# Newton's step as one chain of three operations, operations tied to engines, and a new table of priorities

## The chip, the cores and the metric

The kernel runs on one core of one Trainium2 chip. The core has a matrix engine (PE, with its weight loads PEld), three engines for elementwise work (VectorE = DVE, ScalarE = ACT, GpSimd = POOL), a queue engine (SP) and DMA engines that move data between HBM and the on-chip memory SBUF; PE writes to another memory, PSUM. The metric is the time of one execution in device microseconds, as the median of several runs.

## What is computed

Three layers follow each other: an attention in which a query sees only the keys of its own hash bucket, a gated block with an RMS norm in front, and a second block with a squared ReLU.

```python
# attention: batch 2, 8 heads, 768 positions, 64 wide; proj is 64 x 6
mask = q_bucket[:, :, :, None] == k_bucket[:, :, None, :]   # 6 sign bits of q @ proj and k @ proj
scores = np.where(mask, scale * q @ k.T, -1e9)
attn = np.exp(scores - max); attn = attn / (sum + 1e-9)
x = attn @ v                                                # 1536 tokens x 512
# first block, 512 -> 1536 -> 512
rms = np.sqrt(np.mean(x * x, axis=-1, keepdims=True) + 1e-06)
xn = x / rms * rms_g
x = (silu(xn @ w_gate) * (xn @ w_val)) @ w_out
# second block, 512 -> 2048 -> 512
out = np.maximum(x @ w_in, 0) ** 2 @ w_out
```

## The kernel before

**Precision and tiles.** Every fp32 factor is held as a high and a low part, and three matmuls (high x high, high x low, low x high) make one product; the `L1164` and `L1277`/`L1291` matmuls are those of the two blocks. The attention has 96 slots, one for each head and each 128 queries: `st_S` (scores, L643, four matmuls of 384 columns), `st_min` (L654, DVE: copies the scores out of PSUM and takes the row's maximum `m`), `st_bias` (L663 on ACT, L665 on DVE: one number per row, `b` from `m`), `st_exp` (L672, ACT), then the high and low halves of the weights, transposed, and `st_PV` (L717). Slots of kind `a` (tiles `Pa`, `hla`, `Ta`) make the high half by `st_hi` (a cast to fp16 in the helper `copy`, L381 on ACT or L383 on DVE), the low half by `st_lo` (helper `sub`, L390, POOL or DVE), and are transposed by a DMA (`st_T`, tile `Ta`). Slots of kind `x` (`Px`, `Tx`) are transposed on PE (`st_TP`, L691).

**The norm.** Slots 0 to 47 are the first batch. Its 768 tokens stand in `xall` in two halves of three tiles (`hf` 0 and 1). For each half `plan_norm` lays out: `squares` (sum of squares into `ss`), `power` (DVE L969, then a power of -0.5 on POOL, L974, into `rr`), four Newton operations (L981, L983, L985, L989, all on DVE, on tiles of 128x3), `scales` (L995 ACT, L997 DVE, L999 POOL), four transposes on PE (`x_pe`, L1007) and for each of them `x_hi` (L1017 ACT, L1019 DVE) and `x_lo` (L394, DVE) into `xT`. Only then can the first product of the gated block, `in_pe`, start. The second batch (slots 48 to 95) goes on while the products of the first run, and its own norm comes later.

**What sets the order.** No order is written by hand. `plan_all` registers 3158 operations with what they read, write and hold, with the engines that may do them (`D`, `A`, `P`, `S`, `T` for PE) and a cost for each; `Plan.run` then takes the operation that can start first by its own estimates, and among equals the one of the lowest rank. A cost that is a pair has a second number: a handicap for that engine. `Plan.shift` moves each rank by an entry of a packed table, `SHIFTS`. `port` says that an operation is kept from running beside one of POOL (or DVE) that has it too. Each engine then runs its operations strictly in the planned order.

The code of the functions that the change touches:

Of the kernel before, what the change touches and what calls it, by code (L numbers as in the profile page):

```python
# [112 lines left out]
H_ACT = 3.0  # L113


SHIFTS = (
# [5 lines left out]
    'wo%0>g<5FG_|LA-xDeSW1?}g(p$GAi@BNL%W&8`Q63s;uUKn|1B-3a%lx)<$R<q?(wi(BIFRPlqquv_6Xy+6kZI_XE_z'
    '82LXl*XCZ#t9A66%te59N50eT&^^HCZ8_>fEIhoiFi2YmvxiFU2^q48Jfp(@nG=;-<n_d?F@NW-Vk5<$dU^@<|%%4{_)'
    'c9>@3buMCg=TrX4%O@!O5EwpFEtQF~FmbY$Nrz5jejiO1gPwj+3dNlGynyP;4gvih{)g(>2hKtAO9J)e2*2ja7v?6<vM'
    '7vRpY;JGo)!?QWZ-1o*@?&_H=;@4i_PVZU2`CY2i(E+NEukkWD?6%X)+0NeJ>Um8u?x^y8shu419k!$XEm}5*qiP*HHV'
    '%-cb%5@W<K2Bik8?V?bh}j?I@oL547XXLd_;)cq1sJCgi*KYD;;<(zIRTvOP#|;#`FZY7%VZHS{aw4O3{JiYWR(-|AVR'
    'rlR$B9^0U`<9YI&v)WiG_c&end?fV>UQO?6*W-uz1@Ac5J=LAp_Ev$u-0xaQvaL#LIy<7zFqRl?{14SrxEkpoONp>Pz{'
    'pSw`E{0~?#Q}EFLX~{mcKdITrG^M`YL~Q^$sbJnJ~|7>$7#HmdUz$FW4o%)ZOHq1oDx4hO<l$+6Vj_)hDRDvCfqyn#hI'
    'hsQXuzXKzz&<!mDbrHDgDJXs*qJtbH@_8vQr9MMB-$xgYqv4Lz7G>}b=!MLi}r_Dq)M8s8Fd@FAA2>My(k;!tD%cGT$d'
    'AOSWhU+A5&3oxB(M!=*&((ev^<+g<4yuv*?$WLW?n+o{R1Bf*$TfNv*Mo_4o_i-=Lf-QnqNT+-ZNEyF{XGNm$NDj?yLQ'  # L130
    'i8R=IFz-(2w!0(t{n+1+3J8vErjHCkPB-SR#)_RFqPb7xt-&`Iyw&@>o;v(W}^jrb5sqCV)9D6gfsYMDRz*P}b~oNObW'
    ';Y!wEw1$+oK7=Q_i%d6CQ7AYW&LS%P#yM|7aSWB$+M#iw_2xk*FOcPn)z0GbC{t|;1_N>8CmEwZ!y#`<s7oLTRnV07Hz'
    'wMHs2u$RGS8*C7L(H?j!c!SojYDPS_CKYdF`ooJ&@sAWEOZ2!+2BprM+A4?SHJb3ycnwhFS7}Gt<?_@24HCp;TD|{NLF'
    '%%)yXv#gVQ4fVJCN3nN)I+0-878lo3i&FMm`Ad=z#$$r<m2>JF_*F?Q9?Q5l4@vOXjL0hRKDq;rh-tt{%yZw#1j+TVFG'
    '}@Zt9&7)DCb}om)ilqn$*#&dbg!8V1FSt}zS)!h=+kKr+CnL7vpK?-N=I3XtOl%%O0zDTiN0D^v=!3FnISpLcy2zI-<q'
    'rR^RkbsW;L-)yQPS>&IED-)6_)0tD0tJS>Z@CYjdEFnab7#58|OzNEiLox)UkKR;Vhp6B{0UY9>*)>S4t=ezOjnA24Vp'
    '3l~kWo&-)7EiW2l-jm5DGPk0qMY98^(0q2W$gQn3f0Z>^rZX^7<k*2}*iX&CK(gC9QS?4L<YeL)8e8-^zE=2oNTRY<gz'
    'lqBY;;jZ(W$_1fkSe9Q3WgANpmt~eb$;{yMs)#>);#C2e==3&STZLbfME3a_u&ByH%bo5R>dtP9>ZKC(%=K%L&-AuC1<'
    'I+L6pchFyh3L0LPFTyWhrFBg5p9y<rEr!-HvNI!FFU|Z4ZqLDP0Hjs1iSQH<;Y5DA#^fJ_uIrKO_R&<z-q&0aXo+Fpy='
    'O|*oWcy8vPq*sG;rxX<MStgpSiqC5t}@xK0Mm(We1Hzpmu$Is%RYh#8f}lkjnx=?AAVc7p`A=XRg3+6B(~uo%11{<Dtc'  # L140
    'udBe#r4sEU!oV^JmakPej8$wUo}RrV6p30|NTdY)cgpR6NniVCnFHsR-y6nn9nVT>`F2J)d38iF^fMr?oJh`uNAO1+P6'
    'I_uRs_P0LPD6WHOJ0$RKDixiN42`@I44^+@fl7C>V2ts3MAv^(ZMBl{2Ro^DM>d8IhYrDTB4C3aN50pmG8dGO*q)A_B%'
    'DUP=p&Yo&v|-zDtoKpBhV3b7eApJp0eKFp4&(xIbyz?PPTiz-qZSaH6BW#eAyGn>p!>>QHnNztVEishkEG?T`SQY{5Bb'
    'kR-@J=MIKc5p(ehE63|KP#c`;+8VOg?X;g*G#sS<7$3mhkK!s{9?turQ9%u=?1usNJ=m+)ie*77}tG)*!mx`uPk<>(S_'
    '+zyePUAF{4686g4RE4-g*vM-csqWgW}#PdJa(ZJ+#ROiztIYLN!G<#s4rATSDe3*6qV(>Fd2=+?a(4o)mdfds$8@KwT5'
    'J9FQc3#Hbq{%8fBv<&`xZzSE2H3DEx`qs)MSE#G(;8B3_B#o#}Qy{u<ii*-+UT#QLKXtT}|#NvNap<P_#oBUE=-49~!W'
# [24 lines left out]

class Op:
# [1364 lines left out]
```

## Time and profile before

| | |
|---|---|
| median of 3 runs | 774.93 us (773.62 to 779.03) |
| the profiled execution | 773.52 us, of which the span from first to last instruction is 771.7 us |
| PE | 755.7 us busy (98%) |
| DVE | 652.1 us (84%) |
| ACT | 452.4 us (59%) |
| POOL | 277.7 us (36%) |
| chain that ended last | PE 86%, ACT 5%, DMA 4%, DVE 3% |

The page also cuts the span into 40 slices of 19.3 us; a digit is the busy share in tenths:

```profile
PE   8889998899999999999999999999999999999998
DVE  8989889989898889999889888997669677697765
ACT  5988999979998785636553344466523243232320
POOL 6787877677887574222102121310000000000000
```

The shares are means over two different stages: in the first seven slices all four engines work on the attention; after that PE holds the products of the two blocks.

### The profile page before, as it was taken

How to read it: one execution, taken by the hardware profiler on the slowest of the kernel's cores; microseconds unless marked ns; L12 is line 12 of the kernel's file. 1: busy time of each engine (PE TensorE's matmuls, PEld its weight loads, DVE VectorE, ACT ScalarE, POOL GpSimd, SP SyncE). 2: the span in 40 equal slices, each digit the busy share in tenths (PEclk: the TensorE clock that was granted, in tenths of full speed). 3: DMA queues.
4: the chain of work that ended last, by engine and by line, in shares of the span. 5: the costliest groups of instructions: out<-in, count | busy, mean ns of one | idle time of the engine just before them, and what ended most of it. 6: DMA issues, size and time to landing. Idle time of an engine off the chain costs nothing.

```text
span 771.7 us, 14424 instructions
## 1 busy us (share of the span) xinstructions
PE 755.7 (98%) x5407; PEld 684.2 (89%) x5407; DVE 652.1 (84%) x1301; ACT 452.4 (59%) x871; POOL 277.7 (36%) x244
## 2 busy tenths in 40 slices
PE   8889998899999999999999999999999999999998
PEld 5778897899999999999999999988888888888886
DVE  8989889989898889999889888997669677697765
ACT  5988999979998785636553344466523243232320
POOL 6787877677887574222102121310000000000000
PEclk9999999999999999999999999999999999999999
DMA  8888967698998976333334244313111131111004
GB/s 258 181 184 168 175 139 169 122 231 202 209 216 180 208 162 165 110 133 141 114 119 137 96 142 147 122 60 132 56 55 54 55 110 54 55 55 55 28 1 163
DMA packets 127769, 99.63 MB, mean 129 GB/s; under 512 B 106436, under 2 KB 109460, under 8 KB 127700
## 3 DMA queue, kind: packets, MB, share of 16 engines
q1 hardware_dynamic: 127028, 97.21, 48.6%
q10 hardware_dynamic: 672, 1.51, 0.8%
q8 instruction: 42, 0.69, 0.4%
q14 instruction: 27, 0.22, 0.1%
HBM read 67.12 MB, written 3.15 MB: 91 GB/s over the span
## 4 chain that ended last, share of the span: by engine, by line
PE 86%; ACT 5%; DMA 4%; DVE 3%; issue 1%; POOL 1%; SPq 0%; ACTq 0%; POOLq 0%; DVEq 0%
PE mo L1164 43%; PE mo L1291 17%; PE mo L1277 13%; PE S L643 6%; PE O L717 4%; DMA Ta<-hla 2%; PE mo L528 1%; ACT Px L672 1%; DMA two<-wv 1%; ACT Tx L381 1%; PE mo L691 1%; ACT Pa L672 1%; PE mo L1007 1%; DMA rk<-in_k 1%; ACT hla L381 0%
## 5 line engine op out<-in xcount | busy, mean ns | idle before, releaser
L1164 PE MATMUL mo<-xTA,wih 128*128 128x384 f32 (+1 forms) x512 | 139.1, 353 | 0.0
L1164 PE MATMUL mo<-xTD,wih 128*128 128x384 f32 (+1 forms) x512 | 136.9, 348 | 0.0
L390 POOL TENSOR_TENSOR hla<-Pa,hla 128x768 f16<-128x768 f32 x66 | 110.7, 1681 | 40.8 <-ACT hla L381 29.1
L1308 DVE TENSOR_TENSOR acc<-acc,mo 128x512 f32<-128x512 f32 (+1 forms) x165 | 100.7, 615 | 21.3 <-PE mo L1291 17.7
L1116 DVE SCALAR_TENSOR_TENSOR wv<-wraw,wv 128x512 uint32<-128x512 uint32 x164 | 112.5, 694 | 1.3
L1164 PEld LDWEIGHTS mo<-xTA,wih 128*128 128x128 f32 x512 | 93.6, 189 | 5.2 <-DVE xTA L394 0.2
L1164 PEld LDWEIGHTS mo<-xTD,wih 128*128 128x128 f32 x512 | 93.4, 188 | 5.0
L1200 ACT ACTIVATE mt<-mo 128x512 f32<-128x512 f32 x48 | 28.7, 597 | 109.8 <-PE mo L1164 109.7
L1164 PE MATMUL mo<-xTA,wil 128*128 128x384 f32 (+1 forms) x256 | 89.9, 351 | 0.0
L1164 PE MATMUL mo<-xTD,wil 128*128 128x384 f32 (+1 forms) x256 | 89.0, 348 | 0.0
L1094 ACT ACTIVATE wv<-wraw 128x512 f32<-128x512 f32 x104 | 68.9, 669 | 25.0 <-DMA wraw<-in_w 24.8
L654 DVE TENSOR_SCALAR_CACHE_REDUCE Pa<-S 128x768 f32<-128x768 f32 x66 | 62.8, 951 | 6.9 <-PE S L643 6.6
L1204 DVE TENSOR_TENSOR mu<-mt 128x512 f32<-128x512 f32 x48 | 33.2, 692 | 38.1 <-ACT mt L1200 38.1
L1277 PE MATMUL mo<-yh,woh 128*128 128x384 f32 x192 | 64.9, 338 | 0.0
L1277 PE MATMUL mo<-yh,wol 128*128 128x384 f32 x192 | 64.3, 335 | 0.0
L1277 PE MATMUL mo<-yl,woh 128*128 128x384 f32 x192 | 64.3, 335 | 0.0
L672 ACT ACTIVATE Pa<-Pa,b 128x768 f32<-128x768 f32 x66 | 62.1, 942 | 2.0
L643 PE MATMUL S<-k,q 128*128 128x384 f32 x192 | 55.4, 370 | 5.6 <-DVE Pa L654 3.6
L381 ACT CAST hla<-Pa 128x768 f16<-128x768 f32 x66 | 55.0, 835 | 3.4 <-DMA Ta<-hla 2.9
L381 ACT CAST wih<-wv 128x512 fp32r<-128x512 f32 x38 | 23.6, 621 | 50.6 <-DVE wv L1116 50.4
L643 PE MATMUL S<-two 76*128 76x384 f32 x192 | 50.6, 345 | 1.8 <-DMA two<-wv 1.8
L1164 PEld LDWEIGHTS mo<-xTA,wil 128*128 128x128 f32 x256 | 48.5, 189 | 2.5
(162 smaller groups left out, 1822.7 us busy)
## 6 DMA issues: line engine op xcount, KB each, us to landing
wraw<-in_w SPq DMA_DIRECT2D x104, 512.0 KB, 4.0
rk<-in_k SPq DMA_DIRECT2D x14, 384.0 KB, 4.8
vr<-in_v SPq DMA_DIRECT2D x8, 384.0 KB, 5.4
out<-acc SPq DMA_DIRECT2D x11, 256.0 KB, 2.0
rq<-in_q SPq DMA_DIRECT2D x13, 192.0 KB, 4.3
two<-q SPq DMA_DIRECT2D x7, 192.0 KB, 4.5
two<-wv SPq DMA_DIRECT2D x15, 72.0 KB
Ta<-hla SPq DMA_TRANSPOSE x66, 4.0
```

Source lines behind the costliest of these rows:

```text
L381: nc.scalar.copy(out_, in_)
L390: engine[eng].tensor_tensor(out=out_, in0=in0, in1=in1, op=ALU.subtract)
L643: nc.tensor.matmul(sp[:, hf, 0:TB], d[a][0:kr, t * 128:(t + 1) * 128], d[b2][0:kr, hf * TB:(hf + 1) * TB], start=(n == 0), stop=(n == 1),)
L654: nc.vector.tensor_scalar(out=e["P"].rearrange("p (a b) -> p a b", a=2), in0=e["sp"][:, :, 0:TB], scalar1=-1e9 / SCALE, scalar2=None, op0= ...
L672: nc.scalar.activation(e["P"], e["P"], AF.Exp, bias=e["b"], scale=SCALE)
L1094: nc.scalar.activation(t, f32(wst[m]["hi"]), AF.Abs)
L1116: nc.vector.scalar_tensor_tensor(out=t, in0=src, scalar=scalar, in1=t, op0=op, op1=ALU.bitwise_or)
L1164: nc.tensor.matmul(ps, a[:, c * 128:(c + 1) * 128], b2[:, c, :], start=(c == 0 and n == 0), stop=(c == 3 and n == 2),)
L1204: nc.vector.tensor_tensor(out=us["u"], in0=st["t"], in1=st["t"], op=ALU.mult)
L1277: nc.tensor.matmul(po, a[:, dc * 128:(dc + 1) * 128], b2, start=(j == 0 and n == 0), stop=(j == len(fs) - 1 and n == 2),)
L1291: nc.tensor.matmul(po, a[:, tt * 128:(tt + 1) * 128], b2[:, cols], start=(j == 0 and n == 0), stop=(j == len(fs) - 1 and n == 2),)
L1308: nc.vector.tensor_tensor(out=ac[:, cols], in0=ac[:, cols], in1=po, op=ALU.add)
```

## The change

- `newton` was four planned operations (three products and one multiply-add, each of its own), which the planner could put apart on DVE. It is now one planned operation that issues three `scalar_tensor_tensor` instructions behind one another; the other three entries are empty, so that the count of entries stays. Its cost in the plan is 0.55 and `port` is off.
- The table has a third byte for each operation: a way. An operation that has one gets no handicap on that engine and 6.0 on any other. It is a preference: 428 operations have one, and 36 of these stand on another engine in the plan that results.
- `st_bias` may go to POOL (with a handicap of 40, so only where the table ties it there).
- The table of priorities is another one.
- `store` is written in another way and issues the same.

```diff
+LAG = 6.0
 SHIFTS = (
-    'c-rlk=XX}c*1-47oadaUC31lvNGMVzh9VsiLJMH%2m}PAgc=ceAt2=nNC{O!?;QkbCV~c(CV@);rDFsIA~iHgo_5ZhGw'
+    'c-rk(cYGDqw%&ExnMp|KNR=uCK?sH-AVox)#2{c0xL!m+r3g}`7!2VVAc!ae29TmCNN*w_Di@`LC@pj)kO)am%FLNFGk'
...
+    def lag(self, o, eng, c):
+        if o.way:
+            return 0.0 if eng == o.way else LAG
+        return c[1] if isinstance(c, tuple) else 0.0
...
             moved = int.from_bytes(raw[2 * n:2 * n + 2], "little", signed=True)
+            way = raw[2 * count + n]
+            o.way = "TDAPS"[way - 1] if way else None
             o.rank = (round(o.rank * 32) + moved) / 32 + n * 1e-6
...
-                        ) + (c[1] if isinstance(c, tuple) else 0.0)
+                        ) + self.lag(o, eng, c)
...
-            nc.vector.tensor_scalar(
+            engine[eng].tensor_scalar(
                 out=e["b"], in0=e["m"], scalar1=-SCALE, scalar2=math.log(PSC), op0=ALU.mult,
...
-        add(lambda e: st_bias(e, i), i + R_BIAS, r=[("m", i)], w=[("b", i)], A=0.105, D=(0.08, H_B))
+        add(lambda e: st_bias(e, i), i + R_BIAS, r=[("m", i)], w=[("b", i)], A=0.105, D=(0.08, H_B), P=(0.15, 40.0), port=False)
...
-    def newton(eng, hf, step):
+    def newton(eng, hf):
         ts = slice(hf * TT, hf * TT + TT)
-        r, n = rr[:, ts], rt[:, ts]
-        if step == 0:
-            nc.vector.tensor_tensor(out=n, in0=r, in1=r, op=ALU.mult)
-        elif step == 1:
-            nc.vector.tensor_tensor(out=n, in0=n, in1=ss[:, ts], op=ALU.mult)
-        elif step == 2:
-            nc.vector.tensor_scalar(
-                out=n, in0=n, scalar1=-0.5, scalar2=1.5, op0=ALU.mult, op1=ALU.add
-            )
-        else:
-            nc.vector.tensor_tensor(out=r, in0=r, in1=n, op=ALU.mult)
+        r, n, x = rr[:, ts], rt[:, ts], ss[:, ts]
+        stt = nc.vector.scalar_tensor_tensor
+        stt(out=n, in0=r, scalar=-0.5, in1=r, op0=ALU.mult, op1=ALU.mult)
+        stt(out=n, in0=n, scalar=1.0, in1=x, op0=ALU.mult, op1=ALU.mult)
+        stt(out=r, in0=n, scalar=1.5, in1=r, op0=ALU.add, op1=ALU.mult)
...
         for n in range(4):
             add(
-                lambda e, n=n: newton(e, hf, n), R_X, r=[("rr", hf)], w=[("rr", hf)], D=0.08,
-                port=n != 2,
+                (lambda e: None) if n else (lambda e: newton(e, hf)), R_X, r=[("rr", hf)],
+                w=[("rr", hf)], **({} if n else dict(D=0.55, port=False)),
             )
```

Three places show what this does to the order. The first is DVE at the first norm, behind the power of half 0. Before (`rt` and `rr` are Newton's tiles, `Pa,m<-S` is `st_min`, `sc`/`ma` belong to the scale of `v`):

```order
L983 TENSOR_TENSOR rt<-rt,ss 128x3
L961 SCALAR_TENSOR_TENSOR wv,ss<-xall 128x512
L605 RECIPROCAL sc<-ma 128x2
L654 TENSOR_SCALAR Pa,m<-S 128x768
L985 TENSOR_SCALAR rt<-rt 128x3
L969 TENSOR_SCALAR ss<-ss 128x3
L989 TENSOR_TENSOR rr<-rr,rt 128x3
L654 TENSOR_SCALAR Pa,m<-S 128x768
L997 TENSOR_SCALAR xall<-xall,rr 128x512
```

The same place now, from the instruction ahead of Newton's first on:

```order
L599 TENSOR_REDUCE mx<-vr 128x1
L999 SCALAR_TENSOR_TENSOR rt<-rr 128x3
L1000 SCALAR_TENSOR_TENSOR rt<-rt,ss 128x3
L1001 SCALAR_TENSOR_TENSOR rr<-rt,rr 128x3
L408 TENSOR_TENSOR Tx<-mo,Tx 128x384
L554 TENSOR_SCALAR wv<-mo,cst 48x384
L408 TENSOR_TENSOR Tx<-mo,Tx 128x384
L672 TENSOR_SCALAR Pa,m<-S 128x768
```

Newton's chain of half 0 now stands closed behind one other operation after the power; before, its first and last step had thirteen rows between them, and three of half 1's four steps stood ahead of the first `x_lo`. Half 1's chain now stands behind the last `x_lo` of half 0.

The second place is POOL at the same power (`rr<-ss,half`). Before:

```order
L390 TENSOR_TENSOR hla<-Pa,hla 128x768
L974 TENSOR_TENSOR rr<-ss,half 128x3
L390 TENSOR_TENSOR hla<-Pa,hla 128x768 x2
L1100 TENSOR_SCALAR wv<-wv 128x512
L385 TENSOR_SCALAR k_2690<-rk 128x768
```

And now (`b<-m` is `st_bias`, `xall<-xall,rr` is `scales`):

```order
L683 TENSOR_SCALAR b<-m 128x1
L992 TENSOR_TENSOR rr<-ss,half 128x3
L408 TENSOR_TENSOR hla<-Pa,hla 128x768
L1011 TENSOR_SCALAR xall<-xall,rr 128x512
L408 TENSOR_TENSOR hla<-Pa,hla 128x768
L683 TENSOR_SCALAR b<-m 128x1
```

A `st_lo` stands directly behind the power in both. One of the three `scales` of half 0 has come to POOL, ahead of the second `st_lo`, and biases stand between.

The third place is DVE in the second batch, some 70 slots into the attention. Before:

```order
L654 TENSOR_SCALAR Pa,m<-S 128x768
L1189 SCALAR_TENSOR_TENSOR mu<-mt,mo 128x384
L665 TENSOR_SCALAR b<-m 128x1
L390 TENSOR_TENSOR q_3923<-rq,q_3923 64x768
L654 TENSOR_SCALAR Pa,m<-S 128x768
L1194 SCALAR_TENSOR_TENSOR mu<-mu,mo 128x384
```

And now (`hla<-Pa` as a CAST is `st_hi`):

```order
L683 TENSOR_SCALAR b<-m 128x1
L401 CAST hla<-Pa 128x768
L1201 SCALAR_TENSOR_TENSOR mu<-mt,mo 128x384
L672 TENSOR_SCALAR Pa,m<-S 128x768
L408 TENSOR_TENSOR two<-rk,k_3887 128x768
L408 TENSOR_TENSOR q_3892<-rq,q_3892 64x768
L672 TENSOR_SCALAR Pa,m<-S 128x768
L401 CAST hla<-Pa 128x768
```

Casts of `st_hi`, which were all on ACT, now stand on DVE too: 13 in the program, 3 of them ahead of the first `in_pe`.

Counted over the program: of the biases 22 go from ACT to POOL and 14 from ACT to DVE; 13 `st_hi` from ACT to DVE; 15 operations of the weights' conversion (`w_f32`) from DVE to POOL and 3 back. Ahead of the first `in_pe` PE has 56 `st_S` (57 before), and as many `st_PV` (52), `st_TP` (60) and `hash_pe` (10) as before.

## Rows read from the trace of the kernel before

**Rows 1.** The core's span and mean granted clock of PE.
```profile
core 0: 771.7 us, clock 0.993
```

**Rows 2.** Windows: stretch, length, busy us of PE, PEld, DVE, ACT, POOL; PEclk, DMA.
```profile
300.00:320.00 20.00, 20.00 (x168) 19.67 (x167) 19.75 (x45) 12.77 (x27) 7.13 (x9) 1.00 0.24 81
...
54.50:123.30 68.80, 67.92 (x925) 60.67 (x926) 61.87 (x152) 63.39 (x135) 53.37 (x42) 1.00 0.81 172
123.30:139.20 15.90, 11.64 (x143) 9.67 (x140) 15.05 (x40) 14.75 (x30) 12.79 (x10) 0.89 0.78 144
139.20:320.00 180.80, 180.79 (x1679) 174.80 (x1680) 162.25 (x330) 149.81 (x297) 121.40 (x99) 0.99 0.85 181
```

**Rows 3.** Chain that ended last: start us, us, what; from the norm on.
```profile
125.87 4.04 DMA Ta<-hla
...
139.21 0.94 PE S L643 x4
140.15 3.47 PE mo L1164 x12
...
159.29 0.70 PE S L643 x4
...
177.61 2.08 PE mo L1164 x12
...
768.40 0.42 DVE acc L1308
```

**Rows 4.** Timeline of DVE between the power and the first product.
```profile
128.34 0.17 DVE L983 TENSOR_TENSOR rt<-rt,ss 128x3 f32<-128x3 f32 x1
128.43 0.68 DVE L961 SCALAR_TENSOR_TENSOR wv<-xall 128x512 f32<-128x512 f32 x1
...
129.98 1.46 DVE L985 TENSOR_SCALAR rt<-rt 128x3 f32<-128x3 f32 x1
...
134.25 0.48 DVE L997 TENSOR_SCALAR xall<-xall,rr 128x512 f32<-128x512 f32 x1
134.65 0.95 DVE L390 TENSOR_TENSOR two<-rk,k 128x768 fp32r<-128x768 f32 x1
135.51 1.63 DVE L985 TENSOR_SCALAR rt<-rt 128x3 f32<-128x3 f32 x1
...
138.11 0.94 DVE L654 TENSOR_SCALAR_CACHE_REDUCE Pa<-S 128x768 f32<-128x768 f32 x1
...
138.99 1.66 DVE L394 SCALAR_TENSOR_TENSOR xTA<-mo,cst,xTA 128x384 fp32r<-128x384 f32 x3
```

**Rows 5.** Timeline of POOL in the same stretch.
```profile
123.33 0.88 POOL L974 TENSOR_TENSOR rr<-ss,half 128x3 f32<-128x3 f32 x1 [1.65 <-DVE ss L969]
...
129.77 1.64 POOL L390 TENSOR_TENSOR hla<-Pa,hla 128x768 f16<-128x768 f32 x1
...
134.68 2.45 POOL L390 TENSOR_TENSOR hla<-Pa,hla 128x768 f16<-128x768 f32 x1 [2.07 <-ACT hla L381]
```

**Rows 6.** Timeline of POOL and of DVE at the second batch's norm.
```profile
288.54 1.66 POOL L390 TENSOR_TENSOR hla<-Pa,hla 128x768 f16<-128x768 f32 x1 [0.40 <-ACT hla L381]
...
289.60 1.16 DVE L961 SCALAR_TENSOR_TENSOR wv<-xall 128x512 f32<-128x512 f32 x1
```

**Rows 7.** Windows of 5 us around the first product.
```profile
135.00:140.00 5.00, 2.66 (x35) 2.55 (x34) 5.00 (x8) 4.35 (x9) 4.92 (x3) 1.00 0.64 149
140.00:145.00 5.00, 5.00 (x23) 4.80 (x23) 4.39 (x10) 4.43 (x9) 2.50 (x3) 0.66 0.61 131
```

**Rows 8.** Instructions by line (ns min/median/max, first and last start), and ACT's longest wait for DVE.
```profile
L383 DVE CAST k<-rk x2: 554/557/560, 5.1 to 90.0; 128x768 fp32r<-128x768 f32 x2
...
L385 POOL TENSOR_SCALAR ones<-vr x8: 507/512/857, 16.5 to 217.1; 128x384 f16<-128x384 f32 x8
L385 POOL TENSOR_SCALAR k<-rk x5: 824/831/1103, 66.7 to 222.4; 128x768 fp32r<-128x768 f32 x5
...
ACT b L663 <- DVE Pa L654: 14.4, 18, 3.2
```

More of the change, by code (lines that the diff above doesn't have):

```diff
@@ L122 @@
[L122 to L146, printed above, removed]
@@ new lines @@
+    '5wY#o{J&ERd_HLlGEYHv7Q$r^1UU(4F(RdT<?x!Or}Bl-iaN6(<k?p1fLw?C{6%ftszS&ga{#n0>vn994crR)t92W#^a'
+    'bR=CSe_?GDFMIvv4QdUom*$0E<S955))ddNc(xAZi3<F>9T$w$o91?7TWNc^N%g#%-gR-BY?I>TNV-vvC%yP4?@F+`He'
+    'Rn0l!7}2QdIPm@|HK>tFB<Rg*uGvmq(h1>?vLoWpC~e!7c7%o<hG-zBgm!4}(`psq7dp(Y*=Fp_=qccC1;=jInpveOP~'
+    'Yl{dg0>JE0Rcx8hNtx%TE(gRHbTkS6HpKdwP-i;E8WH~JxoGo{TGo8;f{dtd}bGb`$t=!YrLdijs+^Xy}j7QzsR5eXK<'
+    'F%w2qN>&0oy+QjW}vk1JU@cI#=Vdq9tXFe<W1s{yp`FH58?4*9yq2LFe><%GnfvQo)-sseUS<l*kRzfSgE|h=U87^WqJ'
@@ new lines @@
+    '9)U}rn%z!S}3^cshGJ*79TnlLNaR*7cE;10GhqbXX+QgYTxL9iLDG(R++Mdjgia?p&F%R}4T8qA`}(oHGF$in^YB-Glf'
+    'AAHFR_r77fr6l?qx`4Cc^L8iagj3(y8z}A0VvD3t=*XN8aDUj7<z?-Zy0b&xGLQ^gg}q;<cKC+iQ}zqyOK>23gKuLU!^'
+    'Q|=MudNikJ>$)Xfwmfa5}kBr6jNl{$dYi*?};xk(bL7*mt3Vj}_I!$3lPL7aN*{N4u2eXpsMeUb81c=>FTOtE~jd?6uO'
+    '{0c5_?2eIv)1`XU#eZ%eQeoLz)*5gmrc&U$a(v!V;T+(a0!$4<mZ0WNwRJ2k~NL#!h?#f261U?UT5gVj&UO(w^c8o7Uf'
+    '3hyhGF(lZ(h{W}-s#Z8;#u|*PoP|kl$tO-%nl#Lr=lpKOFrDltswP~p5P!Xk!<Gmq(fvsS6F-Lah#=0rIqE6@FkR_EEe'
@@ L169 @@
+    'z~W6{08t*E4#p!=e_cXxNI6lr+m?i-{S2X{zC|A7613dzI&oF3Xk`~PYG3&dxk7X'
 )
@@ L250, in shift @@
     def shift(self):
-        raw = zlib.decompress(base64.b85decode(SHIFTS)) if SHIFTS else bytes(2 * len(self.ops))
-        assert len(raw) == 2 * len(self.ops)
+        count = len(self.ops)
+        raw = zlib.decompress(base64.b85decode(SHIFTS)) if SHIFTS else bytes(3 * count)
+        assert len(raw) == 3 * count
         for n, o in enumerate(self.ops):
             moved = int.from_bytes(raw[2 * n:2 * n + 2], "little", signed=True)
+            way = raw[2 * count + n]
+            o.way = "TDAPS"[way - 1] if way else None
             o.rank = (round(o.rank * 32) + moved) / 32 + n * 1e-6
@@ L1323, in store @@
         halves = ((nc.scalar, slice(0, CUT)), (nc.sync, slice(CUT, DM)))
-        for queue, cols in halves if (blk, NF2 - 1, tt) == LAST else halves[1:]:
-            if (blk, NF2 - 1, tt) != LAST:
-                cols = slice(0, DM)
+        for queue, cols in halves if (blk, NF2 - 1, tt) == LAST else ((nc.sync, slice(0, DM)),):
             queue.dma_start(
```

74 lines of the change are left out of this document (48 added, 26 removed).

## The prediction

> **What bounds the kernel now.** I read the span first: 771.7 us in the profiled execution, whose own time is 773.5 us, so 1.8 us lie around it [rows 1]. Then the windows: between 139.2 and 320 us PE is busy 180.79 of 180.80 us, between 54.5 and 123.3 us DVE, ACT and POOL are busy 61.9, 63.4 and 53.4 of 68.8 us, and between 123.3 and 139.2 us PE fills only 11.6 of 15.9 us [rows 2]. Then the chain that ended last: the reader is to see a ramp in which transposing DMAs, DVE, ACT and POOL alternate, and from the scores at 139.21 us on nothing but PE pieces, one ending where the next begins, up to the last accumulation at 768.40 us [rows 3]. So the time is the moment at which PE becomes dense, about 139.2 us, plus the PE work that is still open then. Work of DVE, ACT or POOL behind that moment costs nothing as long as PE never waits for it. PE's instructions are the same before and after but for their order, so the change can act in three ways only: an earlier or later first `in_pe`, other PE work done ahead of it, and stalls in the dense stretch.
>
> **The way from the power to the first product.** POOL's power of half 0 starts at 123.33 us [rows 5], the first product at 140.15 us [rows 3]: 16.8 us. DVE is the engine that ends it, with the last `x_lo` at 140.65 us [rows 4].
>
> What Newton costs there: the multiply-add L985 took 1.46 and 1.63 us, its neighbours of the same 128x3 shape 0.17 us [rows 4]. The row of POOL says why: the first began at 129.98 us while POOL's `st_lo` ran from 129.77 to 131.41 us, and ended at 131.44 us; the second ended at 137.14 us, 0.01 us behind a `st_lo` that ended at 137.13 us [rows 5]. The instruction is held until POOL's is over.
>
> Is the new chain free of that? Its three instructions read two tiles of SBUF each. Such a one is L961: begun at 289.60 us under a `st_lo` that ended at 290.20 us, it ended at 290.76 us and took 1.16 us [rows 6], against 0.68 us elsewhere [rows 4]. So two-input instructions are held too, and since a `st_lo` stands right behind the power on POOL, the chain will meet one. I count three instructions at 0.17 us, 0.5 us, plus a hold of 1.5 us for the first (most of a `st_lo` of 1.64 us); the bounds are 0.5 us without a hold and 0.5 + 3 x 1.64 = 5.4 us if each met one of its own. Behind that `st_lo` POOL's next instruction is a `scales` that waits for the chain, so the second and third meet none.
>
> The Trainium skill says of this, in "Advanced Engine Details and Errata", section "VectorE Performance Modes", that GpSimd and Vector instructions that use both read ports block each other. By that sentence alone, three two-input instructions would not be held, and the sum below would be 1.5 us less. "GPSIMD Engine Reference", section "Key points", names Vector instructions with two SBUF inputs beside those; the trace agrees with this one, by the 1.16 us of L961 [rows 6].
>
> DVE between power and last `x_lo`, new against old: the two L985 go (-3.1 us), five small steps of some 0.1 us each between starts go (-0.5), one `st_min` fewer (-0.95), one `split_k2` fewer (-0.95), one `squares` fewer (-0.7), one `scales` fewer (-0.45), two `x_hi` more at the 0.55 us of a `x_lo` (1.66 / 3) (+1.1), the new chain (+0.5) and its hold (+1.5) [rows 4, 5]: -3.5 us. The `st_hi` cast of slot 53 stands behind the last `x_lo`.
>
> Two more paths have to follow, or DVE waits. ACT: 30 instructions in 14.75 us, 0.49 us each [rows 2]; the order has six fewer, -2.9 us. POOL and its DMA: the last `st_PV` ahead of the first product is slot 51's. POOL's row up to its `st_lo` is power 0.88, `st_lo` 1.64, the wait for Newton until about 3.0 us, `scales` 0.6, `st_lo` 1.64, a bias, a weight's step 0.6, a cast of `k` 0.8 and the `st_lo` 1.64, some 8.5 us [rows 5, 8]; a transposing DMA of 4.04 us [rows 3] and the products give 13.1 us. The three end 13.3, 13.9 and 13.1 us behind the power, where the old one took 16.8 us. I take 13.5 us: **-3.3 us**, with bounds 0 (one of the three late by what the chain loses) and -5 us (no hold).
>
> **Ahead of the power.** Counting the order by engine up to the power: ACT loses 17 biases at 0.1 us and two casts, net some -2.4 us; DVE gains two `st_hi` and a `st_lo`, net some +2.4 us; POOL loses 3 to 4 us of `q`, `v` and `st_lo` work and gets 16 biases. No row has a bias on POOL. POOL's one-input instructions take 512 ns for 384 and 831 ns for 768 columns [rows 8], which leaves some 0.2 us for one column; the power on 3 columns took 0.88 us [rows 5]. I take 0.2 us, 3.2 us in all; even at 0.88 us the 14 us fit in POOL's 15.4 us of idle time [rows 2], though each then holds what is queued behind it. What they save is ACT's standing at a bias until DVE has the maximum: 14.4 us in 18 waits over the program [rows 8]; but the `st_exp` behind still wants the same number. ACT was the fuller engine there (63.4 against 61.9 us [rows 2]) and they trade places: **0 us**, bounds -2.4 and +2.4.
>
> **What is left for later.** One `st_S` fewer stands ahead of the first product: **+0.7 us** [rows 3].
>
> **The dense stretch.** Between the first and the 36th product DVE gets ten casts of `st_hi` (0.56 us each by the cast of `k` [rows 8]), ten biases, three `st_lo`, and gives away `squares`, `scales`, `x_lo` and weight steps: net some +4 us. The casts were planned as if POOL never held them; by POOL's 121 of 181 us [rows 2] two thirds of them would meet a `st_lo`, half of 1.64 us each: +5.5 us. DVE had 18.5 us idle there [rows 2], so 9.5 us fit on average; they don't where it was full already, 19.75 of 20 us at 300 us [rows 2]. **+0.5 us**, bounds 0 and +9.5. Newton's later chains and the other form of the store cost nothing: PE's queue covers the first, and the second issues the same DMAs.
>
> **Sum.** 773.5 - 3.3 + 0.7 + 0 + 0.5 = 771.4 us on the profiled execution's time. That time lies 1.4 us under the median of the three runs, which spread by 5.4 us; by the median the sum is 772.8. I forecast **772 us**.
>
> **Rivals.** *(1) The ramp ends where it did.* The three paths lie within a microsecond of each other, so any one being late takes the gain: a transposing DMA of over 7 us instead of 4.04, or DVE's 2.4 us ahead of the power. For it: the chain shows DVE, ACT and DMA taking turns. Then 773.5 + 0.7 = 774.2, or up to 776 us. *(2) Slower: DVE becomes the bound in the dense stretch.* Its place is 280 to 340 us, where it is all but full; it decides once casts and their holds exceed what was idle there. Price: up to 9.5 us, against a gain of 2.6: 776 to 781 us, 783 at worst with rival 1. Against it: PE lost nothing there with DVE at 90%. *(3) More.* PE's first twelve matmuls took 3.47 instead of 2.08 us and the scores 0.94 instead of 0.70 [rows 3], with a granted clock of 0.66 at 140 to 145 us, part of it at 1.2 instead of 2.4 GHz, behind 5 us in which PE was busy 2.66 [rows 7]. A shorter hole may keep 2.4 GHz: -1.6 us. With ACT's 2.4 us and no hold (-1.5): 766 to 769.5 us.
>
> **How the numbers follow.** Forecast (769.5 to 774 us) 0.48, rival 1 0.18, rival 2 0.14, rival 3 0.20. The range 766.5 to 778.5 us leaves out about half of rival 3's lower end and half of rival 2. A measurement here tells 1%, 7.7 us, from no change: faster than 767.2 us takes some 0.12 out of rival 3, slower than 782.7 us 0.05 out of rival 2; the rest, 0.83, is within.
>
> **What would show it.** The first L1164 matmul at 136 to 137.5 us; Newton's three instructions within 2.5 us, the first long and ending with a `st_lo`; biases on POOL at about 0.2 us; PE without gaps from there on. Wrong would be: a PE wait behind 140 us, a first `st_PV` ahead of `in_pe` that waits for `Ta`, or a power later than 125 us.

## The result, and the profile after

The changed kernel is slower: median 785.32 us (782.43 to 786.58, four runs) against 774.27 us (772.33 to 779.03) of the kernel before on the same chips, a ratio of 1.013 with a 95% interval of 1.0093 to 1.0166. The forecast was 772.0 us, the range 766.5 to 778.5. The profiled execution of the changed kernel took 786.58 us, with a span of 784.8 us.

| | before | after |
|---|---|---|
| span | 771.7 us | 784.8 us |
| first `in_pe` matmul | 139.99 us | 139.96 us |
| span behind it | 631.7 us | 644.8 us |
| PE | 755.7 us (98%) | 761.8 us (97%) |
| DVE | 652.1 us (84%) | 669.8 us (85%) |
| ACT | 452.4 us (59%) | 439.0 us (56%) |
| POOL | 277.7 us (36%) | 286.3 us (36%) |

The first matmul of the first product, before and after (start us, us):

```profile
139.99 0.51 PE L1164 MATMUL mo<-xTA,wih 128*128 128x384 f32 x2
```

```profile
139.96 0.59 PE L1176 MATMUL mo<-xTA,wih 128*128 128x384 f32 x2
```

In these two executions the whole difference of 13.1 us arises behind the first product, where the prediction expected nothing but dense PE work. The span of the changed kernel, and the same windows as in [rows 2, 7] (stretch, its length, then busy us of PE, PEld, DVE, ACT and POOL with instruction counts; PEclk; DMA share; GB/s):

```profile
core 0: 784.8 us, clock 0.989
```

```profile
139.20:320.00 180.80, 172.08 (x1570) 163.85 (x1571) 165.30 (x320) 129.83 (x237) 116.23 (x97) 0.98 0.86 175
```

```profile
140.00:145.00 5.00, 2.29 (x17) 1.97 (x12) 4.93 (x6) 1.66 (x2) 4.84 (x3) 1.00 0.47 90
145.00:150.00 5.00, 3.87 (x17) 3.81 (x18) 3.08 (x7) 4.20 (x7) 2.54 (x3) 0.66 1.01 126
185.00:190.00 5.00, 3.16 (x41) 3.05 (x42) 4.22 (x9) 4.43 (x8) 4.28 (x4) 0.74 1.18 303
```

PE is busy 172.08 of 180.80 us where it was busy 180.79 before [rows 2]: 8.7 us of waits. Beside the longest of them the granted clock is lower: 0.66 behind the hole of 140 to 145 us and 0.74 at the hole of 185 us, so part of that work runs at 1.2 instead of 2.4 GHz. The kernel before had one such stretch, 0.66 behind its own hole ahead of 139.2 us [rows 7]. What PE waited for between 139 and 325 us (sum, times, longest):

```profile
PE S L661 <- DVE Pa L672: 6.1, 5, 3.8
PE O L735 <- DMA Ta<-hla: 2.7, 4, 1.8
```

In the kernel before, the same view of the same stretch has one row, a `st_S` waiting 2.3 us for `st_min` at the very start. The longest wait of the changed kernel stands right behind the first product:

```profile
146.13 0.73 PE L661 MATMUL S<-k,q 128*128 128x384 f32 x2 [3.84 <-DVE Pa L672]
```

The chain that ended last, there (start us, us, what):

```profile
140.80 0.90 DVE hla L401
141.70 1.70 DVE rt L999
143.40 0.02 issue
143.42 0.17 DVE rt L1000
143.62 1.49 DVE rr L1001
145.11 0.89 DVE Pa L672 x2
145.99 0.14 issue
146.13 1.37 PE S L661 x4
```

This is Newton's second chain (half 1), between the `st_hi` cast of slot 53 and `st_min` of slot 55. DVE and POOL side by side (start us, us, engine, line, operation):

```profile
140.72 0.98 DVE L401 CAST hla<-Pa 128x768 f16<-128x768 f32 x1
141.62 1.76 DVE L999 SCALAR_TENSOR_TENSOR rt<-rr 128x3 f32<-128x3 f32 x1
143.42 0.16 DVE L1000 SCALAR_TENSOR_TENSOR rt<-rt,ss 128x3 f32<-128x3 f32 x1
143.62 1.49 DVE L1001 SCALAR_TENSOR_TENSOR rr<-rt,rr 128x3 f32<-128x3 f32 x1
145.03 0.94 DVE L672 TENSOR_SCALAR_CACHE_REDUCE Pa<-S 128x768 f32<-128x768 f32 x1
```

```profile
139.63 1.66 POOL L408 TENSOR_TENSOR hla<-Pa,hla 128x768 f16<-128x768 f32 x1
141.36 2.00 POOL L408 TENSOR_TENSOR q<-rq,q 64x768 fp32r<-64x768 f32 x1
143.45 3.25 POOL L408 TENSOR_TENSOR hla<-Pa,hla 128x768 f16<-128x768 f32 x2
```

The reader is to see two ends that agree and one start. The first instruction of the chain begins 0.26 us into POOL's `q` and ends with it (143.38 and 143.36 us). The second begins 0.03 us ahead of POOL's next instruction and takes 0.16 us. The third begins 0.17 us into that `st_lo`, one of two that take 3.25 us together, 1.63 us each, and ends when it does (145.11 and 145.08 us). Three instructions worth 0.5 us take 3.5 us. All the while PE has run out: the one product that its order has there, the twelve matmuls of 139.96 us, was over at 142.3 us, and the next in its order is a `st_S` that stands behind `st_min` of slot 55. The Trainium skill says of the port that DVE and POOL share, in "SBUF — State Buffer", section "SBUF: two separate sides", that whoever starts first has it for the whole instruction and the other is blocked; the trace agrees, by these ends and by the 0.16 us of the one that started first.

The theory to be tested was therefore: **one block on DVE, the second closed chain under POOL's holds, starves PE**. The rivals: the `st_hi` casts on DVE; the biases on POOL, which would make the transposes and so `st_PV` late; the new order as such; the new form of the step.

### The profile page after: what moved, and what is told of

Read it like the earlier page. It is cut to its first block, busy times and chain, and to the rows that moved or that the text cites. A ratio compares the mean times of both kernels' runs of the same rounds, so it can differ in the third digit from the quotient of the medians.

```text
span 784.8 us, 14382 instructions
## 1 busy us (share of the span) xinstructions
PE 761.8 (97%) x5407; PEld 686.7 (88%) x5407; DVE 669.8 (85%) x1313; ACT 439.0 (56%) x809; POOL 286.3 (36%) x275
## 4 chain that ended last, share of the span: by engine, by line
PE 75%; DVE 10%; DMA 7%; ACT 4%; issue 2%; POOL 2%; SPq 0%; POOLq 0%; DVEq 0%; ACTq 0%
PE mo L1176 38%; PE mo L1303 17%; PE mo L1289 12%; DMA Ta<-hla 5%; PE S L661 4%; PE O L735 3%; DVE Pa L672 2%; DVE Px L672 2%; DMA two<-wv 1%; ACT hla L399 1%; DVE Tx L408 1%; PE mo L546 1%; DMA rk<-in_k 1%; ACT Tx L399 1%; ACT Pa L690 1%
## 5 line engine op out<-in xcount | busy, mean ns | idle before, releaser
L408 POOL TENSOR_TENSOR hla<-Pa,hla 128x768 f16<-128x768 f32 x62 | 103.2, 1668 | 34.2 <-ACT hla L399 25.2
L408 POOL TENSOR_TENSOR wol<-wv,woh 128x512 fp32r<-128x512 f32 x10 | 13.3, 1333 | 108.6 <-ACT woh L399 84.6
L403 POOL TENSOR_SCALAR wih<-wv 128x512 fp32r<-128x512 f32 x10 | 6.8, 682 | 126.0 <-DVE wv L1128 125.3
```

Of the source, the lines that this page charges most:

```text
L408: engine[eng].tensor_tensor(out=out_, in0=in0, in1=in1, op=ALU.subtract)
```

## Experiments

Ratios are to runs of the kernel before on the same chip, with 95% intervals; the changed kernel itself stands at 1.013. The chips differ: the median of the kernel before was 774.27 us beside the changed kernel and 776.17 to 777.55 us beside the experiments. So the ratios are to be compared, and an expectation in microseconds is to be read as a ratio to 774.27. The column "second chain" is the time from the first instruction of Newton's second chain to the end of its last in the profiled execution, where it is closed and on DVE.

| kernel | ratio | interval | second chain |
|---|---|---|---|
| changed kernel | 1.0130 | 1.0093 to 1.0166 | 3.49 us |
| e1_form (old order, new form) | 0.9957 | 0.9933 to 0.9982 | open |
| e2_hi (casts on ACT) | 1.0060 | 1.0031 to 1.0090 | 2.50 us |
| e3_bias (biases on ACT) | 1.0113 | 1.0061 to 1.0164 | 3.49 us |
| e4_chain (chain behind `st_min` 55) | 1.0077 | 1.0052 to 1.0101 | 1.40 us |
| e5_two (e2 and e4) | 1.0105 | 1.0074 to 1.0135 | 2.74 us |
| e6_order (new order, old engines) | 1.0215 | 1.0191 to 1.0239 | 2.66 us |
| e7_engines (old order, new engines) | 1.0348 | 1.0319 to 1.0378 | open |
| e8_pool (Newton on POOL) | 1.0040 | 1.0011 to 1.0069 | on POOL |
| e9_pool_hi (e8 and e2) | 1.0041 | 1.0013 to 1.0069 | on POOL |
| e10_pool (old order, Newton on POOL) | 0.9991 | 0.9964 to 1.0017 | on POOL |
| e11_closed (old order, closed chain) | 1.0025 | 1.0006 to 1.0044 | 0.56 us |
| e12_half1 (second chain alone on POOL) | 1.0047 | 1.0023 to 1.0071 | on POOL |
| e13_again (e1 once more) | 0.9968 | 0.9943 to 0.9994 | open |
| e14_free (nothing on POOL that holds the chain) | 1.0019 | 0.9995 to 1.0043 | 0.98 us |

### The parts, each by itself

**e1_form**: the new form of Newton's step alone.

```diff
     # the kernel before; steps 0, 1 and 3 stay where they were, step 2 issues nothing
-    nc.vector.tensor_tensor(out=n, in0=r, in1=r, op=ALU.mult)
+    stt(out=n, in0=r, scalar=-0.5, in1=r, op0=ALU.mult, op1=ALU.mult)
-    nc.vector.tensor_tensor(out=n, in0=n, in1=ss[:, ts], op=ALU.mult)
+    stt(out=n, in0=n, scalar=1.0, in1=ss[:, ts], op0=ALU.mult, op1=ALU.mult)
-    nc.vector.tensor_scalar(out=n, in0=n, scalar1=-0.5, scalar2=1.5, op0=ALU.mult, op1=ALU.add)
-    nc.vector.tensor_tensor(out=r, in0=r, in1=n, op=ALU.mult)
+    stt(out=r, in0=n, scalar=1.5, in1=r, op0=ALU.add, op1=ALU.mult)
```

> The kernel before with Newton's three-instruction form alone: step 0, 1 and 3 at their old places of the old order, step 2 empty, the old table, no ways. In the kernel before L985 was held twice by POOL (1.46 and 1.63 us) ahead of the first product; the new form has none of it there, but its three two-input instructions can each meet a hold. Theory 'the form is the loss': 780 us or more. Theories that put the loss on place, casts, biases or order: 772 to 774.5 us, ratio to the kernel before 0.997 to 1.000.

773.39 us, ratio 0.9957: the form is not the loss, it comes out as a small gain. At the places where the old order has the steps, none of the six instructions of the first batch is held; the last step of each half, from DVE's timeline:

```profile
131.72 0.15 DVE L986 SCALAR_TENSOR_TENSOR rr<-rt,rr 128x3 f32<-128x3 f32 x1
...
141.23 0.16 DVE L986 SCALAR_TENSOR_TENSOR rr<-rt,rr 128x3 f32<-128x3 f32 x1
```

The same instruction on the same tiles takes 0.15 us or 1.49 us, by what POOL does when it begins.

**e2_hi**: the 13 casts back on ACT, order kept.

```diff
         for o in plan.run():
+            if "st_hi" in o.fn.__code__.co_freevars:
+                o.eng = "A"
             o.fn(o.eng)
```

> The changed kernel, its order kept, with the 13 st_hi casts that had gone to DVE put back on ACT. Theory 'casts make DVE the bound in the dense stretch' (13 x 0.56 us plus some 2.6 us of holds between 140 and 325 us): most of the loss comes back, 775 to 778 us. Theory 'one block, Newton's second chain ahead of st_min 55': only the one cast in that block is taken out, 0.98 us, so 783 to 785 us. Theory 'biases on POOL' or 'the order itself': 783 us or more.

781.40 us, ratio 1.0060: half of the loss comes back, less than the theory of the casts wanted (1.001 to 1.005) and more than a single 0.98 us. The trace shows why the two theories aren't clean here: without the cast in front of it the chain begins while POOL still runs the `st_lo` before, so its held instructions take 0.59 and 1.67 us instead of 1.76 and 1.49, and `st_min` of slot 55 begins 3.6 us behind the first product (142.32 less 138.70) instead of 5.1 (145.03 less 139.96). PE's waits of 139 to 325 us:

```profile
PE O L735 <- DMA Ta<-hla: 4.1, 3, 2.3
PE S L661 <- DVE Pa L672: 3.9, 3, 2.2
```

The wait for `st_min` is smaller, the one for the transposes larger.

**e3_bias**: the same edit with `st_bias` in place of `st_hi`.

> The changed kernel, its order kept, with every bias on ACT (36 had gone to POOL or DVE, some more stood on DVE before). Theory 'biases on POOL delay exp, st_lo and the transposes, so that st_PV waits for Ta (2.7 us of PE waits, four of them)': 780 us or less. Theories of the chain, of the casts or of the order: 784 to 787 us, since ACT then waits at a bias for DVE's maximum as before.

787.22 us, ratio 1.0113: no different from the changed kernel. The biases on POOL are not the cause; waits for the transposes are there without them too (3.0 us against 2.7).

**e4_chain**: `st_min` of slot 55 ahead of the block.

```diff
-        for o in plan.run():
+        order = plan.run()
+        for n in (914, 851):   # st_hi of slot 53, Newton of half 1
+            o = plan.ops[n]
+            order.remove(o)
+            order.insert(order.index(plan.ops[930]) + 1, o)   # behind st_min of slot 55
+        for o in order:
```

> The changed kernel with one place of its order changed: on DVE st_min of slot 55 goes ahead of Newton's second chain (three instructions, 3.4 us with holds) and of the st_hi cast of slot 53 (0.98 us). Theory 'one block': PE's wait of 4.05 us at 142 to 146 us and the half clock behind it (some 1.7 us) go, 779 to 781 us. Theory 'casts' or 'order': the gap is only moved, since DVE stays behind through 140 to 310 us, 784 us or more.

783.45 us, ratio 1.0077: the 779 to 781 us of the first theory are 1.006 to 1.009, so it holds by the ratio, but the mechanism is not quite as told. `st_S` waits less now (0.38 us at 143 us), but the chain, still held for 1.01 us, is later, and the next to wait is PE's transposition `x_pe` of half 1, for ACT's scales behind the chain (1.7 us at the longest):

```profile
PE mo L1019 <- ACT xall L1007: 1.9, 2, 1.7
PE S L661 <- DVE Pa L672: 1.9, 3, 1.3
```

So two kinds of work on PE wait for the block: `st_S` by way of `st_min`, and `x_pe` by way of the scales. Changing the place makes the wait shorter and changes who waits.

### Order against engines

**e5_two** is e2 and e4 together.

> The changed kernel with the 13 casts back on ACT and st_min of slot 55 ahead of Newton's second chain, both at once. Each alone gave back 0.7 and 0.5 points of the 1.3. Theory 'two separate causes on DVE': they add, ratio to the kernel before 1.000 to 1.003, 775 to 778 us. Theory 'the order itself is tight, and a stall cured at one place comes back at the next': 1.005 or more, 779 us or more, with waits of st_S and st_PV between 160 and 225 us still there.

784.60 us, ratio 1.0105: no better than either, and the intervals of the three overlap. The gains don't add, and the longest wait is not at another place of the order. It is the same block again: the chain is held for 1.02 and 1.49 us, ACT's scales and with them `x_pe` are late by 3.0 us.

```profile
PE mo L1019 <- ACT xall L1007: 3.0, 1, 3.0
PE O L735 <- DMA Ta<-hla: 2.3, 2, 2.1
PE S L661 <- DVE Pa L672: 1.5, 2, 1.3
```

**e6_order** and **e7_engines** cross the two parts of the table: an order with the other kernel's engines for all 197 operations that differ.

```diff
+ENG = ( '68P 71A 79P ...' )   # operation and engine
...
         order = plan.run()
+        for x in ENG.split():
+            plan.ops[int(x[:-1])].eng = x[-1]
```

> The changed kernel's order of operations with the engines of the kernel before: all 197 operations that stood on another engine go back to where they were (biases, casts, weight steps, scales and the rest); Newton's closed chain stays. Theory 'engines': the loss goes but for the closed chain, ratio 1.000 to 1.005. Theory 'order': the loss stays, ratio 1.008 or more.

> The converse: the kernel before with its order and its four Newton steps, and the 197 operations on the engines of the changed kernel. Theory 'engines': the loss is here, ratio 1.008 or more. Theory 'order': 0.997 to 1.004, 773 to 778 us. An order made for other engines can cost something of its own in either of the two; if both are slower than the changed kernel, order and engines belong together and neither is the cause alone.

793.29 us (1.0215) and 803.81 us (1.0348). Both are slower than the changed kernel, the case that the expectation had named: order and engines belong together, and neither half of the table can be called the cause by itself. The runs say nothing more.

### Newton away from DVE

**e8_pool**: the changed kernel with the step on POOL.

```diff
-        stt(out=n, in0=r, scalar=-0.5, in1=r, op0=ALU.mult, op1=ALU.mult)
-        stt(out=n, in0=n, scalar=1.0, in1=x, op0=ALU.mult, op1=ALU.mult)
-        stt(out=r, in0=n, scalar=1.5, in1=r, op0=ALU.add, op1=ALU.mult)
+        nc.gpsimd.tensor_tensor(out=n, in0=r, in1=r, op=ALU.mult)
+        nc.gpsimd.tensor_tensor(out=n, in0=n, in1=x, op=ALU.mult)
+        nc.gpsimd.tensor_scalar(out=n, in0=n, scalar1=-0.5, scalar2=1.5, op0=ALU.mult, op1=ALU.add)
+        nc.gpsimd.tensor_tensor(out=r, in0=r, in1=n, op=ALU.mult)
```

> The changed kernel, its order kept, with Newton's step on POOL as four small instructions (three products, one multiply-add) right behind POOL's power. So nothing of it stands on DVE and no POOL instruction can hold it. POOL pays four instructions of 0.35 to 0.54 us each, by its biases. Theory 'holds of the closed chain': the 3.4 us block ahead of st_min 55 goes from DVE, PE's wait of 4.05 us at 142 us shrinks to about 1 us, 780 to 783 us. Theory 'the place of the cast and the order matter, not the chain': 784 to 787 us.

779.00 us, ratio 1.0040: 0.9 of the 1.3 points come back, more than expected. **e12_half1** does this for half 1 of the first batch alone:

```diff
+        if late or hf == 0:
             stt(out=n, in0=r, scalar=-0.5, in1=r, op0=ALU.mult, op1=ALU.mult)
             stt(out=n, in0=n, scalar=1.0, in1=x, op0=ALU.mult, op1=ALU.mult)
             stt(out=r, in0=n, scalar=1.5, in1=r, op0=ALU.add, op1=ALU.mult)
+            return
+        nc.gpsimd.tensor_tensor(out=n, in0=r, in1=r, op=ALU.mult)
...
```

> The changed kernel with only the second chain (half 1 of the first batch) on POOL; the first chain and the two of the second batch stay on DVE. Newton on POOL for all four gave back 0.9 points, some 7 us: 3 us of it by an earlier first product (136.9 instead of 140.0 us), the rest by the gap at 142 us. Theory 'the second chain is the gap, the first chain the ramp': here only the gap goes, first product at 139 to 140 us, ratio 1.006 to 1.009, 780 to 783 us. Theory 'only the second counts and the earlier ramp was chance': 1.003 to 1.005.

779.64 us, ratio 1.0047: nearly as much. So the second chain is what counts; the first chain (held once in all these kernels, for 1.03 us or so) and the two of the second batch are worth nothing that these runs can tell. The wait that remains for `st_min`:

```profile
PE S L661 <- DVE Pa L672: 2.2, 3, 1.3
```

Of these only 0.71 us stand at 141 us; the 1.3 us are at 164 us. The cast of slot 53 keeps its place here and is held as before, and `st_min` follows it at once, 2.0 us behind the first product (140.01 less 137.98) instead of 5.1:

```profile
139.09 1.00 DVE L401 CAST hla<-Pa 128x768 f16<-128x768 f32 x1
140.01 0.94 DVE L672 TENSOR_SCALAR_CACHE_REDUCE Pa<-S 128x768 f32<-128x768 f32 x1
```

**e9_pool_hi** adds e2 to e8.

> The changed kernel with Newton on POOL and the 13 st_hi casts back on ACT. Alone these gave 1.004 (from 1.013) and 1.006. Theory 'two causes that add': 0.997 to 1.000, 772 to 775 us at the kernel before's 774 to 777. Theory 'both act on the same gap at 142 us (the cast of slot 53 stands in that block too), and what is left is the order, with st_S pairs that have no product between them at 162 to 170 us': 1.002 to 1.006.

781.83 us, ratio 1.0041: moving the casts brings nothing once the chain is gone. In the trace it is an exchange: the waits for `st_min` fall from 3.6 us in e8 to 2.1 us, those for the transposes rise from 0.6 to 4.7 us. That the gain of e2 was the shorter block fits with this; it was not tried by itself.

**e10_pool** and **e11_closed** put Newton on POOL, or as the closed chain on DVE, into the old order at the place of the old first step.

```diff
         # the kernel before
+        if step:
+            return
+        nc.gpsimd.tensor_tensor(out=n, in0=r, in1=r, op=ALU.mult)   # e10: these four on POOL
...
+        stt(out=n, in0=r, scalar=-0.5, in1=r, op0=ALU.mult, op1=ALU.mult)   # e11: these three on DVE
...
```

> The kernel before with its four Newton steps on POOL, closed behind POOL's power, all else as it was. By the kernel before the two holds of L985 (1.46 and 1.63 us) go, and rr is ready some 2 us behind the power (four instructions of 0.2 us). Theory 'Newton's way sets the ramp': first product 2 to 3 us earlier, ratio 0.996 or less. Theory 'the ramp has other limits, Newton only counts where it holds up DVE right ahead of a st_min': 0.997 to 1.001.

776.29 us, ratio 0.9991: no difference. In the old order Newton's way is no limit that this run can tell. The interval reaches down to 2.8 us of gain, so the two held L985 of [rows 4], 3.1 us in all, were not wholly on the path.

> The kernel before with Newton as the closed chain of three instructions on DVE, at the place of its old first step; old order, old table. This separates closing the chain from the new table. Theory 'a closed chain costs by itself, since each instruction meets POOL': 1.004 or more, with three to six long instructions. Theory 'it costs only where POOL happens to run st_lo and where DVE has a st_min waiting behind': 0.995 to 1.002, since at the old places POOL was between instructions (in the open form all six took 0.15 to 0.17 us).

779.40 us, ratio 1.0025, against 0.9957 of the same three instructions at open places: closing the chain at the place of the first step costs 0.6 (by e13) to 0.7 points in the old order as well; the ratio lies between what the two theories wanted. One of its six instructions is held, and what stands behind it on DVE meets POOL at other moments, up to a `split_k2` ahead of the last four `x_lo` that takes 2.41 instead of 0.95 us [rows 4]:

```profile
129.15 1.63 DVE L984 SCALAR_TENSOR_TENSOR rt<-rt,ss 128x3 f32<-128x3 f32 x1
...
139.77 2.41 DVE L390 TENSOR_TENSOR two<-rk,k 128x768 fp32r<-128x768 f32 x1
```

### Holds or place

What was left open was whether the chain is dear because of POOL's holds or because of its place ahead of `st_min`. **e14_free** keeps place, form and engine and takes away what holds it: the cast, on which POOL's next `st_lo` waits, goes behind `st_min`, and POOL's `split_q2` goes to DVE behind it.

```diff
+        order = plan.run()
+        for n in (234, 914):   # split_q2 of head 11, st_hi of slot 53
+            o = plan.ops[n]
+            order.remove(o)
+            order.insert(order.index(plan.ops[930]) + 1, o)   # behind st_min of slot 55
+        plan.ops[234].eng = "D"
+        for o in order:
```

> The changed kernel with Newton's second chain on DVE at its place ahead of st_min 55, but with nothing on POOL that could hold it: the cast of slot 53, on which POOL's next st_lo waits, goes behind that st_min, and POOL's split_q2 of head 11 goes to DVE, behind it too (0.95 us). The chain then meets only the end of one st_lo. Theory 'the holds are the price of the chain': chain done within 1 us, PE's wait at 142 us under 1.5 us, ratio 1.003 to 1.007 as with the second chain on POOL. Theory 'its place in the order is the price': 1.009 or more.

778.99 us, ratio 1.0019, and the interval reaches 1. DVE's timeline and, behind it, POOL's:

```profile
140.69 0.59 DVE L999 SCALAR_TENSOR_TENSOR rt<-rr 128x3 f32<-128x3 f32 x1
141.31 0.17 DVE L1000 SCALAR_TENSOR_TENSOR rt<-rt,ss 128x3 f32<-128x3 f32 x1
141.51 0.16 DVE L1001 SCALAR_TENSOR_TENSOR rr<-rt,rr 128x3 f32<-128x3 f32 x1
141.59 0.95 DVE L672 TENSOR_SCALAR_CACHE_REDUCE Pa<-S 128x768 f32<-128x768 f32 x1
```

```profile
139.59 1.67 POOL L408 TENSOR_TENSOR hla<-Pa,hla 128x768 f16<-128x768 f32 x1
143.10 4.76 POOL L408 TENSOR_TENSOR hla<-Pa,hla 128x768 f16<-128x768 f32 x2 [1.84 <-DVE hla L401]
```

The first instruction meets the end of one `st_lo`, the others find POOL idle; `st_min` begins at 141.59 instead of 145.03 us. PE still waits there, but 0.62 us and not 3.84; its longest waits, 1.4 us each, are now further on:

```profile
139.20:320.00 180.80, 175.44 (x1610) 167.11 (x1608) 170.48 (x331) 133.95 (x246) 119.21 (x100) 1.00 0.86 184
```

```profile
142.70 0.58 PE L661 MATMUL S<-k,q 128*128 128x384 f32 x2 [0.62 <-DVE Pa L672]
```

```profile
PE S L661 <- DVE Pa L672: 3.5, 4, 1.4
PE O L735 <- DMA Ta<-hla: 1.7, 2, 1.4
```

So what the chain costs are the holds and not its place: with the chain on the same engine at the same place, the wait behind the first product falls from 3.84 to 0.62 us, and 1.1 of the 1.3 points are gone. The edit moves the cast and `split_q2` as well; e12, in which the cast stays and only the chain leaves DVE, brings `st_min` forward nearly as far and gives nearly as much, while the cast alone (e2, e9) gives less. It is not the whole loss behind the first product: that part took 631.7 us before and 644.8 us after, and takes 638.6 us here, 639.3 in e12 and 639.7 in e8. So the held chain is worth 5 to 6 of the 13.1 us; the rest is taken up below, under what stays open.

**e13_again** repeats e1 on another chip.

> The kernel before with Newton's three instructions at the old places, once more and with more rounds, since it came out ahead of both kernels. If that was real: 0.994 to 0.998 with an interval under 1. If it was chance: an interval that holds 1.

775.29 us, ratio 0.9968: faster than the kernel before by 0.3 to 0.4% in both measurements, with both intervals under 1. It is the only part of the change that these runs show to be a gain. Where the gain arises they don't show: behind the first product the two profiled executions took 631.7 and 631.4 us, as the kernel before did.

## Why the prediction was wrong

- **The time is the dense moment plus the open PE work.** The frame held as bookkeeping and failed as a forecast: the dense moment came as before (139.96 against 139.99 us), and the 13.1 us lie behind it. 8.5 us are waits (the 8.7 less 0.2 that stand ahead of the first product), 0.7 us is the one `st_S` more by the forecast's own term, and the rest, some 3.9 us, is PE work that took longer. As an estimate from the granted clock of windows of 5 us, the changed kernel loses 3.4 us behind its holes (0.66, 0.74 and 0.92 at 145, 185 and 190 us) and the kernel before lost 1.7 us (0.66 at 140 us), so the clock makes 1.7 of the 3.9 us; where the others go stays open.
- **The step that failed** is the sentence that closes the dense stretch: "Newton's later chains and the other form of the store cost nothing: PE's queue covers the first". The working of the first chain had the mechanism and its price, one hold of 1.5 us, and was right to 0.6 us (2.0 us told, 1.4 us measured). It wasn't asked for the second chain, whose place behind the last `x_lo` was known. What PE's order has there is one product, 2.1 us by [rows 3]. What stood on DVE between the last `x_lo` and the end of `st_min` was the cast 0.56, the chain 0.5, `st_min` 0.94 us, and up to four instructions that POOL can hold: 5.2 us in the run. The cover was 2.1 us, and this could have been set side by side. The term beside it, 0.5 us for the whole dense stretch, failed too: with the chain freed (e14) that part is still 6.9 us longer than before. There too PE waits, for `st_min` and for transposes, and why the new order has less cover there is shown only in part (see what stays open).
- **Rival 2**, DVE as the bound in the dense stretch, named the engine and the mechanism and missed place and price: not 280 to 340 us, where DVE is full, but 142 us and again between 165 and 197 us, where DVE's average has slack and PE's order has nothing else to do. Its price of up to 9.5 us came from the casts; e9 shows that moving them back gives nothing without the chain, and e12 that the chain is worth 0.8 points, some 6 us. "PE lost nothing there with DVE at 90%" was the wrong evidence against it: a share over 180 us says nothing about a stretch of 5 us.
- **The first chain and the ramp.** The first instruction took 1.03 us, held by a `st_lo`, the others 0.16 us, and the chain was done 2.1 us behind the power's end: as told. From the power to the first product it took 14.5 us, where 13.5 was forecast and 16.7 measured before. The gain of 2.1 us was there and was eaten by the next point.
- **Rivals 1 and 3.** In the profiled run the ramp did end where it did before (rival 1), but the loss isn't there. The clock that rival 3 wanted to keep was kept at 140 to 145 us (1.00) and lost behind the new hole (0.66).
- **Ahead of the power, 0 us with bounds of 2.4.** Here 125.42 against 123.33 us, +2.1, inside the bounds. Over all runs this moment scatters by as much: 122.25 to 125.80 us in the kernels with the new order, 123.33 to 127.43 us in those with the old one and its engines. No cost of the order can be read from one such number.
- **The bias on POOL, 0.2 us**: the median of the 22 is 190 ns, the longest 836. Right, and by e3 they neither cost nor bring anything that these runs can tell.

```profile
L683 POOL TENSOR_SCALAR b<-m x22: 190/190/836, 13.2 to 306.6; 128x1 f32<-128x1 f32 x22
```

- **What would be wrong**: all three signs came. A PE wait behind 140 us is what the trace showed first; the last `st_PV` ahead of `in_pe` waited 0.32 us for `Ta`; and the power, at 125.42 us, was later than 125 us. The sign of being right, a first product at 136 to 137.5 us, did not come.

**What stays open.** With the chain freed (e14), the span behind the first product is 638.6 us (778.3 less 139.72), 6.9 us more than before. The profile puts 5.2 us of it down to PE's waits, the longest of them ending at about 166, 182 and 191 us. The first of these is there in all ten kernels with the new order: the `st_S` of slot 61 follows directly on that of slot 60, with no product between. The new order has three such pairs up to slot 63, the old one none, and by slot 63 seven products stand ahead in the new order where ten stood in the old. That the missing products are the cause was not tried, and it may not be all: in the changed kernel the product that comes next needs a low part of its weight that DVE finished at 171.51 us, 1.5 us behind the end of the wait. Against this stands the ramp, which seems to gain: the first product comes at 136.9 to 141.0 us in the ten kernels with the new order, at 139.8 to 142.7 us in the four with the old order and its engines whose chain isn't closed on DVE. The ratio of e14 asks for such a gain: 1.0019 is 1.5 us, though 6.9 us more lie behind the first product of its profiled execution, so by this estimate some 5 us would have to be gained ahead of it, and that one execution shows 0.3 us (139.72 against 139.99). Nor is it settled why order and engines of one kernel do so badly with those of the other (e6, e7).

## What to carry to other kernels

- A chain of tiny instructions on DVE has no fixed price: each can cost the rest of the POOL instruction under which it begins. Count them one by one against POOL's queue at that place, and for every chain that a change closes, not for the first alone.
- Ask of each closed block how much ready work PE has in that moment, in us, and who waits behind the block (here two: `st_S` by `st_min`, `x_pe` by the scales). Shares over a stage don't answer it.
- When a cure at one place gives half and two cures together give no more than one, look whether they change the same block; taking away the suspected wait itself (e14) told more than moving it.

## What the runs showed of the hardware

- The hold goes by who starts first, to 0.03 us: L1000 began that much ahead of POOL's next instruction and took 0.16 us; its neighbours began 0.26 and 0.17 us too late and took 1.76 and 1.49 us. So a small shift changes which instructions are held: in e2 the chain begins 0.9 us earlier against POOL's `q`, and its first instruction takes 0.59 instead of 1.76 us, its third 1.67 instead of 1.49 us.
- POOL can be the one that waits: in e10 its last Newton step began at 138.35 us under a `split_k2` of DVE that ended at 139.08 us, ended at 139.14 us, and took 0.79 us where it took 0.19 us free.
- POOL's small instructions of 128x3 are nearly as quick as DVE's when free: 0.19 to 0.21 us each in e8, against 0.15 to 0.17 us on DVE, where the power on the same three columns takes 0.88. Newton's four steps behind the power, from DVE to POOL (e8, POOL's timeline):

```profile
124.71 0.21 POOL L998 TENSOR_TENSOR rt<-rr 128x3 f32<-128x3 f32 x1
125.00 0.19 POOL L999 TENSOR_TENSOR rt<-rt,ss 128x3 f32<-128x3 f32 x1
125.29 0.19 POOL L1000 TENSOR_SCALAR rt<-rt 128x3 f32<-128x3 f32 x1
125.56 0.19 POOL L1001 TENSOR_TENSOR rr<-rr,rt 128x3 f32<-128x3 f32 x1
```

- A long wait of PE can cost more than its length: behind the hole from 142.3 to 146.1 us the granted clock is 0.66, and the scores take 1.37 us where they take 0.70 in [rows 3], part of it at 1.2 instead of 2.4 GHz. Not every wait does: in e14, where the longest is 1.4 us, the granted clock of 139.2 to 320 us is 1.00.
